# A pooled-attention and maxout kernel: one third of the key folds as a tensor_reduce on VectorE, and a new hand-written order of all steps

## The chip, the cores and the metric

The kernel runs on one core of a Trainium2 chip. The metric is the device time of one execution in microseconds (us), median of the runs shown. The profile is one further execution, taken by the hardware profiler; its span runs from the first to the last instruction. TensorE's granted clock was 1.000 of full speed over the profiled span.

## The reference, cut to what matters

Keys and values are averaged over groups of 8 tokens, so that 576 tokens attend to 72 pooled keys; the attention output goes through a maxout layer of three weights and an output projection.

```python
k_p = k.reshape(B, H, Sp, pool, D).mean(axis=3)     # B=8, H=8, S=576, pool=8, Sp=72, D=64
v_p = v.reshape(B, H, Sp, pool, D).mean(axis=3)
scores = scale * np.matmul(q, k_p.transpose(0, 1, 3, 2))
attn = softmax(scores)                               # over the 72 pooled keys
x = np.matmul(attn, v_p)  -> [4608 tokens, 512]
h = np.maximum(np.maximum(x @ w1, x @ w2), x @ w3)   # 512 -> 768
out = h @ w_out                                      # 768 -> 512
```

## The kernel before, in words

Two streams are interleaved. The **attention stream** goes batch by batch (8 batches of 576 tokens), the **maxout stream** goes in blocks of 512 tokens (9 blocks, 0 to 8). Batch b+1 is attended to while block b goes through the maxout layer, since a block needs the tokens of its batch.

For a batch, Pool (GpSimd) issues the loads of k, q and v (`load_k` L79, `load_q` L99, `load_v` L91). The average over 8 tokens is made as a "fold": three additions that halve the 8 neighbours each time, 8 to 4 (L163), 4 to 2 (L165), 2 to 1 (L167). For batch 1 VectorE folds the keys (`fold_k(b, nc.vector)`), for batches 2 to 7 Pool does, and Pool folds the values of all batches but the first. The folded keys `kp` are transposed on TensorE (`keys`, tile `pkt`, L202) and copied to `kz` by VectorE and ScalarE (`turn_k`, L213). The queries are transposed on TensorE (tiles `pqt`, L195) for batches 0 to 2, and by one DMA transpose on SP's queue (step `T`, L349, into `qT`) for batches 3 to 7. Scores (L226, tiles `psc` and `psf`) go to ScalarE for exp (L231). `values` multiplies with the folded values (tile `pav`, L302), and VectorE normalises (reciprocal L310, product L312, tile `xn`). `turn_x` transposes `xn` into the ring `xT`: on TensorE (tile `pxt`, L293) for batches 0 to 2, by DMA transposes on SP's queue (L287) from batch 3 on.

For a block, `hidden` makes 12 pieces of 4 matmuls (tile `pw`, L419); ScalarE evicts the first of each pair with relu (L425), VectorE the second with a max (L427, tile `hT`). From block 1 the output projection is done with seven products in the place of eight (`out_seven`, L765, tiles `oA`, `oB`, `oC`); its sums of token and hidden tiles are made by VectorE (`sums_of`, L664, tile `tt`), and its evictions by ScalarE (L776) and VectorE (L779). From block 6 the maxout matmuls use the same scheme (`seven`, L842), on weight sums `sw` made earlier by VectorE (`fold_w`, L588 and L597).

The order on every engine is the order in which the program's steps are written out. After block 0 there are two kinds of hand-written lists: `MIDDLE`, one string for each of blocks 1 to 5, and `ORDER`, one string for the rest, run by `weave`. The steps are:

- `h-` and `h+`: the matmuls of the next piece of the block's hidden layer, and its eviction. `-` begins a step and `+` ends it, for all steps; a step without a sign is both.
- `1` to `7` with `-`, `+`: the seven output products (10 matmuls each); `a1` to `a4`, `b1` to `b4`: their sums on VectorE. `f`: one weight sum of `fold_w`. `S`: one sum of output weights (L649).
- `q0` to `q3`, `T`, `k`, `s0`, `s3`, `s6`, `v0` to `v4`, `x0` to `x4`: the attention steps above, of the next batch if no batch is named; `4:T` names batch 4.
- `q4<`, `k4<`, `v4<`: Pool issues a load, behind the last hidden matmuls and the last `T` written so far. `k4+2`, `v3+2`: Pool does the next two steps of a fold. `!`: the next fold step is held until VectorE's last difference of a weight or tile sum has ended.
- In `ORDER`, `1a` is product 1 of the maxout scheme for part a of the block, `o1` an output product, `s70` a score step of batch 7, `v62` and `x62` value steps of batch 6; `b1` to `b4` and `F`, `T`, `H`, `h` are sums and projection pieces.

Where it matters for the prediction: the load of batch 7's queries is `q7<`, its DMA transpose `7:T`, and the first score that reads it `s70`.

Of the kernel before, what the change touches and what calls it, by code (L numbers as in the profile page):

```python
# [14 lines left out]
def kernel(  # L15
# [141 lines left out]
    def fold_steps(e, t, out, dtype=F32, parts=1):  # L157
        part, n = t.shape[:2]
        f = const.tile([part, n, 4, D], dtype, name="half" if dtype == F32 else "halfh",
                       tag="half" if dtype == F32 else "k16")  # L160
# [177 lines left out]
    def do(b, steps):  # L338
# [3 lines left out]
        for name in steps.split():  # L342
# [530 lines left out]
    fold_k(2, nc.gpsimd)  # L873
# [5 lines left out]
    def pool_step(n, name):  # L879
# [69 lines left out]
    MIDDLE = {  # L949
        1: """  # L950
            h- q4< k4< h+ 1:x2 1:v4- h- h- v4< h+ 1:v4+ h+ h- 1:x3 h- h+ h+ h- 1:x4 h+ h- k-
            h- h+ h+ q0 h h- k+ h+ h q1 h s0- s0+ s0+ q2 h- s0+ h- s0+ h+ b1 S q3 h+ h- S S
            3:T S h+ a3 s3- a1 s3+ s3+ h- s3+ h- h+ h+ a2 h- s3+ a4 s6- s6+ 1- s6+ h+ b3 b2
            b4 v0 2- 1+ 6- x0 v1 7- v2- 6+ x1 5- 2+ 7+ v2+ ! k3+4 v3- v3+2 v3+ 5+ v4 3- x2
            4- x3 3+ 4+ x4
        """,
        2: """
            h k5< k- h- k+ h+ a1 a3 h- a2 f a4 f ! v3+2 v5< h+ f s0- s0+ s0+ s0+ h- h- h- h+
            h+ s0+ h- h+ s3- h+ h- f s3+ h- s3+ h+ h- s3+ b1 s3+ s6- h+ s6+ h- h+ h- s6+ !
            k4+2 h+ h+ b2 b3 b4 ! k4+2 1- 4:T v0- 1+ v1- v0+ x0 2- v1+ 6- v2- 7- x1 2+ 7+  # L960
            v4+2 6+ v2+ 5- v3- 5+ v3+ x2 x3 v4 x4 3- 4 3+
        """,
        3: """
            k- q5< k+ a3 k6< h a1 h- h- h+ a2 s0- f a4 ! v4+2 s0+ s0+ f h- h+ s0+ h+ s0+ h-
            h- h+ h+ s3- h- v6< h+ h s3+ s3+ s3+ s3+ h- b1 h- h+ h+ s6- s6+ ! k5+2 h h- s6+
            1- h+ b2 b3 b4 1+ ! k5+2 v5+2 v0- 2- v0+ x0 v1 6- 2+ x1 6+ 7- 5:T 7+ v2- 5- v2+
            x2 v3- 5+ v3+ v4 x3 3 x4 4
        """,
        4: """
            h- q6< h+ k- h- k+ a1 a2 f h+ h- a3 a4 ! v5+2 h- f h+ k7< h+ s0- s0+ h- h- s0+  # L970
            s0+ h+ s0+ h+ 6:T h- s3- h+ s3+ s3+ s3+ h- s3+ h+ h- b1 h+ h ! k6+2 s6- s6+ h h
            b3 b2 b4 s6+ ! k6+2 1- v6+2 v0 2- 1+ x0 v1- 6- v1+ 2+ x1 v2 7- 6+ 5- x2 v3 6:k-
            x3 7+ 5+ 3- 6:k+ v4 x4 4- 3+ 4+
        """,
        5: """
            h q7< a1 v7< h- a2 h- a3 h+ h+ a4 ! v6+2 h- s0- s0+ h+ s0+ h- s0+ s0+ h- h- k7+4
            h+ h+ s3- h+ 7:T s3+ h- s3+ h- s3+ s3+ h+ s6- h+ s6+ s6+ h h- v0 h+ h- x0 v1- h+
            v1+ x1
        """}
    folds = iter([f for wi in range(1, 3) for f in [fold_w(wi)] * 4])  # L980

    def middle(n):

        pieces, outs, out_tiles = hidden(n), None, project(n)
        for name in MIDDLE[n].split():
            if name[0] == "h":
                parts(name, lambda: next(pieces))
            elif name == "F":
                next(out_tiles)
            elif name == "f":  # L990
                next(next(folds))
# [15 lines left out]
    for n in range(1, 6):  # L1007
        middle(n)
# [50 lines left out]
```

## Time and profile before

| what | value |
| --- | --- |
| time, median of 3 runs | 226.8 us (226.77 to 227.67) |
| profiled execution, its own time | 227.08 us |
| its span, first to last instruction | 225.4 us |
| TensorE matmuls, busy | 212.3 us (94% of the span) |
| VectorE, busy | 161.4 us (72%) |
| ScalarE, busy | 120.3 us (53%) |
| Pool, busy | 140.9 us (63%) |
| instructions | 4876 |

A row of the groups of instructions reads: line, engine, operation, output tile and input tiles, shapes (partitions x elements, type), how many; then busy us in total, mean ns of one; then the engine's idle us just before them and what ended most of it. In the timeline, the first number is the start in us, the second the length, and brackets hold the idle time before and what ended it. A line of the waits reads: engine and tile that waited, what it waited for, then us in total, how often, the longest.

### The profile page before, as it was taken

How to read it: one execution, taken by the hardware profiler on the slowest of the kernel's cores; microseconds unless marked ns; L12 is line 12 of the kernel's file. 1: busy time of each engine (PE TensorE's matmuls, PEld its weight loads, DVE VectorE, ACT ScalarE, POOL GpSimd, SP SyncE). 2: the span in 40 equal slices, each digit the busy share in tenths (PEclk: the TensorE clock that was granted, in tenths of full speed). 3: DMA queues.
4: the chain of work that ended last, by engine and by line, in shares of the span. 5: the costliest groups of instructions: out<-in, count | busy, mean ns of one | idle time of the engine just before them, and what ended most of it. 6: DMA issues, size and time to landing. Idle time of an engine off the chain costs nothing.

```text
span 225.4 us, 4876 instructions
## 1 busy us (share of the span) xinstructions
PE 212.3 (94%) x1884; PEld 147.1 (65%) x1885; DVE 161.4 (72%) x314; ACT 120.3 (53%) x233; POOL 140.9 (63%) x121
## 2 busy tenths in 40 slices
PE   6688999999999999999999999999799999999993
PEld 2477744458658645964685468547589667788882
DVE  3668898036997796776679668729767977878940
ACT  2267524855883576237724842693694445564330
POOL 7974300999939969775885769794292903881020
PEclk9999999999999999999999999999999999999999
DMA  6999999999649999649967999699530755200265
GB/s 179 209 197 197 211 203 209 202 168 230 115 105 156 168 176 247 122 61 214 252 85 154 221 202 151 86 236 166 109 56 19 163 102 113 47 0 3 66 198 159
DMA packets 47303, 33.55 MB, mean 149 GB/s; under 512 B 26992, under 2 KB 42288, under 8 KB 47280
## 3 DMA queue, kind: packets, MB, share of 16 engines
q0 software_dynamic: 16944, 16.98, 47.8%
q1 hardware_dynamic: 29888, 15.87, 31.1%
q10 hardware_dynamic: 448, 0.39, 0.7%
q8 instruction: 15, 0.25, 0.5%
q14 instruction: 8, 0.07, 0.1%
HBM read 34.60 MB, written 9.44 MB: 195 GB/s over the span
## 4 chain that ended last, share of the span: by engine, by line
PE 58%; DMA 17%; DVE 10%; POOL 7%; ACT 3%; issue 3%; ACTq 0%; POOLq 0%; DVEq 0%
PE pw L419 17%; PE oA L765 12%; DMA vt<-in_v_dram 8%; PE oC L765 6%; PE pA L842 5%; DMA mw<-in_moe_w_dram 4%; DMA qT<-qb 4%; PE oB L765 3%; PE pC L842 3%; PE pav L302 2%; PE po L471 2%; PE psc L226 2%; POOL half L163 2%; DVE kz L213 2%; DVE tt L664 1%
## 5 line engine op out<-in xcount | busy, mean ns | idle before, releaser
L419 PE MATMUL pw<-xT,mw 128*128 128x512 f16 (+1 forms) x336 | 68.5, 349 | 0.3 <-ACT xT L296 0.2
L419 PEld LDWEIGHTS <-mw 128*128 128x128 f16 x336 | 30.7, 98 | 26.1 <-issue 1.8
L163 POOL TENSOR_TENSOR half<-vt 72x1024 f32<-72x1024 f16 (+1 forms) x12 | 29.1, 2444 | 20.8 <-DMA vt<-in_v_dram 13.3
L427 DVE TENSOR_TENSOR hT<-t,pw 128x512 f16<-128x512 f16 (+1 forms) x42 | 25.3, 608 | 19.1 <-PE pw L419 11.3
L231 ACT ACTIVATE et<-psc 72x512 f16<-72x512 f32 (+2 forms) x66 | 33.9, 571 | 6.7 <-PE psc L226 6.5
L165 POOL TENSOR_TENSOR half<-half 72x1024 f32<-72x1024 f32 (+1 forms) x13 | 28.1, 2165 | 12.6 <-DVE tt L664 5.2
L425 ACT ACTIVATE t<-pw 128x512 f16<-128x512 f32 (+1 forms) x42 | 22.6, 538 | 15.1 <-PE pw L419 14.5
L312 DVE TENSOR_TENSOR xn<-pav,rcp 128x512 f16<-128x512 f32 x40 | 27.6, 691 | 1.4
L776 ACT COPY osb<-oA 128x512 f32<-128x512 f32 x20 | 11.7, 587 | 20.1 <-PE oA L765 19.9
L851 ACT CAST pad<-pA 128x512 f16<-128x512 f32 x27 | 15.1, 585 | 11.7 <-PE pA L842 9.1
L765 PEld LDWEIGHTS <-tt 128*128 128x128 f16 x200 | 18.8, 98 | 2.1
L163 POOL TENSOR_TENSOR half<-ktFalse 96x768 f32<-96x768 f16 (+1 forms) x11 | 19.3, 1773 | 0.6 <-issue 0.5
L226 PEld LDWEIGHTS <-kz 64*128 64x128 bf16 (+1 forms) x161 | 8.9, 95 | 12.4 <-issue 7.2
L302 PEld LDWEIGHTS <-et 72*128 72x128 f16 x320 | 14.9, 98 | 3.0 <-issue 1.1
L302 PE MATMUL pav<-vp,et 72*128 72x65 f16 x320 | 16.3, 194 | 0.6 <-POOL vp L167 0.3
L310 DVE RECIPROCAL rcp<-pav 128x8 f32<-128x8 f32 x40 | 8.1, 201 | 11.3 <-PE pav L302 11.2
L842 PEld LDWEIGHTS <-sw 128*128 128x128 f16 x144 | 13.8, 98 | 2.7 <-issue 0.2
L822 DVE SCALAR_TENSOR_TENSOR hT<-pad 128x512 f16<-128x512 f16 x18 | 14.0, 785 | 1.1 <-ACT pad L855 0.5
L819 DVE TENSOR_TENSOR pad<-pad,pC 128x512 f16<-128x512 f16 x18 | 12.3, 681 | 3.5 <-PE pC L842 2.7
L226 PE MATMUL psc<-qT,kz 64*128 64x256 bf16 (+5 forms) x138 | 13.3, 263 | 1.0 <-DVE qT L197 0.9
L616 POOL TENSOR_TENSOR pad<-xT 128x256 f16<-128x256 f16 x8 | 5.5, 687 | 13.1 <-DMA xT<-xn 13.1
L765 PEld LDWEIGHTS <-hT 128*128 128x128 f16 x126 | 12.3, 98 | 1.4
(122 smaller groups left out, 400.6 us busy)
## 6 DMA issues: line engine op xcount, KB each, us to landing
out_dram<-osb SPq DMA_DIRECT2D x32, 128.0 KB, 4.6
ktFalse<-in_k_dram POOLq DMA_DIRECT2D x7, 576.0 KB, 9.1
qb<-in_q_dram POOLq DMA_DIRECT2D x7, 576.0 KB, 7.6
vt<-in_v_dram POOLq DMA_DIRECT2D x7, 576.0 KB, 11.8
out_dram<-osb SPq DMA_DIRECT2D x11, 256.0 KB, 6.8
mw<-in_moe_w_dram POOLq DMA_DIRECT2D x9, 256.0 KB, 9.2
ktTrue<-in_k_dram SPq DMA_DIRECT2D x3, 384.0 KB, 5.1
out_dram<-ob SPq DMA_DIRECT2D x8, 128.0 KB, 2.9
```

Source lines behind the costliest of these rows:

```text
L163: yield e.tensor_tensor(out=f[:, at], in0=t[:, at, 0:4, :], in1=t[:, at, 4:8, :], op=ALU.add)
L165: yield e.tensor_tensor(out=f[:, :, 0:2, :], in0=f[:, :, 0:2, :], in1=f[:, :, 2:4, :], op=ALU.add)
L226: nc.tensor.matmul(out, kz_all[b % 2][f % 2][rows, h, :], qTs[b][rows, n + i0:n + i1, 64 * (h % 2):64 * (h % 2) + 64], start=True, stop=True)
L231: nc.scalar.activation(out=out, in_=in_, func=FT.Exp, scale=1.0 / 64.0)
L302: nc.tensor.matmul(pav[:, h // 4, 65 * (h % 4):65 * (h % 4) + 65], ets[b][:, h, c0:c0 + 128], vp_all[:, b, h, :], start=True, stop=True)
L312: nc.vector.tensor_tensor(out=xn, in0=pv[:, :, :, 0:D], in1=rcp.to_broadcast([128, 2, 4, D]), op=ALU.mult)
L419: mm = nc.tensor.matmul(pw, w_sb[wi][:, kc, bass.ts(jc, 128)], x[:, kc], start=(kc == 0), stop=(kc == KCH - 1))
L425: yield lambda t=t, pw=pw: nc.scalar.activation(out=t, in_=pw, func=FT.Relu)
L427: yield lambda t=t, pw=pw: nc.vector.tensor_tensor(out=hT[:, jc, c0:c1], in0=t, in1=pw, op=ALU.max)
L765: nc.tensor.matmul(p, left, right, stop=(r == 4), skip_group_check=True, start=(i in FIRST and r == 0 and (m == 0 or n == LAST)))
L842: mm = nc.tensor.matmul(p[:, w], a[:, kc, bass.ts(g, 128)], b[:, kc, :], start=(i in FIRST and w + kc == 0), stop=(w + kc == 2), skip_grou ...
L851: nc.scalar.copy(out=kept(i, g), in_=p)
```

## The change

1. A new function `reduce_k` makes the pooled keys of two of the six key rows per partition (`i` 0 and 1 of 6) with one VectorE instruction, a `tensor_reduce` over the 8 neighbours, 96 x 1024 elements in, 96 x 128 out. It is called as step `K0` for batches 2 to 7. Pool's fold of those batches covers the other four rows, in 3 instructions (96 x 1024, 96 x 512, 96 x 256 elements written) where there were 4 (for batch 2, where there were 3, also 3).
2. `MIDDLE` becomes one list for blocks 1 to 5. A step names its block (`3/h-`) or batch (`4:T`), so that steps of neighbouring blocks may stand between each other. All its steps stand in a new order, and 3 of the key fold steps stand behind a `!` where 7 did.
3. `ORDER` is written anew: the same steps in another order.

The matmuls are the same in number and shape. Block 0 and all that comes before the first `MIDDLE` step are the same, but for Pool's fold of batch 2.

```diff
+    def reduce_k(b, i0, i1):
+        if b not in kps:
+            new_kp(b)
+        with nc.allow_low_precision(reason="summed in f32, rounded once as stored"):
+            nc.vector.tensor_reduce(out=kps[b][:, i0:i1],
+                                    in_=kts[b][:, i0:i1].rearrange("p i j d -> p i d j"),
+                                    op=ALU.add, axis=mybir.AxisListType.X)
...
+            elif name[0] == "K" and b > 1:
+                reduce_k(b, 2 * i, 2 * i + 2)
...
-    fold_k(2, nc.gpsimd)
+    fold_k(2, nc.gpsimd, 2, 6)
...
-                folding[what, b] = fold_steps(nc.gpsimd, kts[b], kps[b], parts=2)
+                folding[what, b] = fold_steps(nc.gpsimd, kts[b][:, 2:6],
+                                              kps[b][:, 2:6], parts=1)
...
     ORDER = """
-        b1 o1- 2a- b3 o1+ k7- b2 1a- 1b- v62- 1a+ k7+ 2a+ b4 T o6- s70- o6+ o2- s70+ o2+ 6a-
...
+        b1 o1- 1a- b3 b2 k7- v62- o1+ k7+ b4 1b- 1a+ 2a- T 2a+ o6- o2 7a 6a- 1b+ o6+ s70 v62+
...
-        2: """
-            h k5< k- h- k+ h+ a1 a3 h- a2 f a4 f ! v3+2 v5< h+ f s0- s0+ s0+ s0+ h- h- h- h+
-            h+ s0+ h- h+ s3- h+ h- f s3+ h- s3+ h+ h- s3+ b1 s3+ s6- h+ s6+ h- h+ h- s6+ !
-            k4+2 h+ h+ b2 b3 b4 ! k4+2 1- 4:T v0- 1+ v1- v0+ x0 2- v1+ 6- v2- 7- x1 2+ 7+
-            v4+2 6+ v2+ 5- v3- 5+ v3+ x2 x3 v4 x4 3- 4 3+
-        """,
-        3: """
-            k- q5< k+ a3 k6< h a1 h- h- h+ a2 s0- f a4 ! v4+2 s0+ s0+ f h- h+ s0+ h+ s0+ h-
...
-        5: """
-            h q7< a1 v7< h- a2 h- a3 h+ h+ a4 ! v6+2 h- s0- s0+ h+ s0+ h- s0+ s0+ h- h- k7+4
...
+    MIDDLE = """
+        2:q0 1/h- 2:K0 1/h+ v4< q4< k4< 1:v4- 1:x2 3:T 1/h 1:v4+ 1/h- k3+1 1/h+ 1:x3 1/h 2:k-
...
+        2/b4 v4+2 3:v0+ 2/6- 3:v1- q5< 3:v1+ 2/6+ 3:x0 2/7 2/2+ 3:v2- 3:x1 2/5- 3:v2+ 3:v3-
+        3:v4- 3:x2 2/5+ 3:v3+ 3:v4+ 2/3 2/4- 4:k- 3/a3 3/h- 3/a1 3/h- 3/h+ 4:k+ 3/h- k6< 3/a2
...
+        5:s6+ 4/1+ 4/b4 4/2- 5:v0 4/6 5:v1- 5:x0 5:v1+ 4/2+ 5:v2 4/5- 5:v3- ! k6+2 5:v3+ 4/7-
+        v6+2 q7< 5:v4- 5:x1 4/5+ 4/7+ 5:x2 5:v4+ 4/3- 5:x3 4/4- 6:k- 5/h- 6:k+ 4/4+ 5/h- 5/h+
+        5/h- ! v6+2 7:K0 5/h+ v7< k7+1 5/a1 6:s0- 6:s0+ 5/h+ 6:s0+ 6:s0+ 5/a2 5/h- 5:x4 6:s0+
+        7:T 5/h+ 5/h 5/h- 6:s3- 6:s3+ 6:s3+ 5/h+ 5/a3 6:s3+ 5/h- 5/h- 6:s3+ 5/h+ 6:s6- 6:s6+
...
```

More of the change, by code (lines that the diff above doesn't have):

```diff
@@ L158, in fold_steps @@
         part, n = t.shape[:2]
[L159 to L160 removed]
+        f = const.tile([part, 6 if part == 96 else n, 4, D], dtype, name="half" if dtype == F32 else "halfh",
+                       tag="half" if dtype == F32 else "k16")[:, 0:n]
         for i in range(0, n, n // parts):
@@ L991, in middle @@
+    """
+    folds = iter([f for wi in range(1, 3) for f in [fold_w(wi)] * 4])
+    def middle():
+        pieces, outs = {}, {}
+        for name in MIDDLE.split():
+            n, _, step = name.rpartition("/")
+            n = int(n or 0)
+            if step[0] == "h":
+                if n not in pieces:
+                    pieces[n] = hidden(n)
+                parts(name, lambda: next(pieces[n]))
+            elif step == "f":
                 next(next(folds))
-            elif name == "!":
+            elif step == "S":
+                next(out_sums)
+            elif step == "!":
@@ L1004, in middle @@
-        assert next(pieces, None) is None
+            elif n and step[0].isdigit():
+                if n not in outs:
+                    outs[n] = out_seven(n)
+                parts(name, lambda: outs[n](int(step[0]), 0, 1))
+            elif step[0] in "ab":
+                sums_of(n, step)
+            elif step[2:3] == "<" or step[2:3] == "+" and step[3:]:
+                pool_step(step)
+            else:
+                b, _, step = step.rpartition(":")
+                do(int(b), step)
@@ L1006 @@
+        assert all(next(p, None) is None for p in pieces.values())
     tt_all.append(const.tile([128, 4, 5, HALF], F16, name="tt", tag="tt"))
-    for n in range(1, 6):
-        middle(n)
+    middle()
     assert next(folds, None) is None
```

82 lines of the change are left out of this document (32 added, 50 removed).

## The prediction

> **What bounds the kernel now.** I read the busy shares first, then TensorE's busy time by stage, then what TensorE waited for, then the timeline at its gaps.
>
> ```profile
> PE 212.3 (94%) x1884; PEld 147.1 (65%) x1885; DVE 161.4 (72%) x314; ACT 120.3 (53%) x233; POOL 140.9 (63%) x121
> ```
>
> TensorE's matmuls fill 94% of the span, so a faster fold can't pay by itself: Pool (63%) and VectorE (72%) are not the bound. Only TensorE's idle time can be won. The busy time by stage says where that lies (each line: stage and its length, then matmuls, weight loads, VectorE, ScalarE, Pool, each with its instructions, granted clock, DMA share, GB/s):
>
> ```profile
> 45.00:60.00 15.00, 14.50 (x157) 10.37 (x154) 9.61 (x23) 8.85 (x19) 14.60 (x10) 1.00 0.99 189
> 60.00:80.00 20.00, 19.66 (x189) 13.37 (x187) 17.01 (x32) 12.76 (x26) 15.95 (x12) 1.00 0.73 136
> 80.00:100.00 20.00, 19.85 (x172) 13.02 (x170) 16.27 (x33) 9.48 (x19) 16.36 (x12) 1.00 0.80 155
> ...
> 155.00:160.00 5.00, 3.40 (x40) 2.84 (x38) 4.13 (x9) 2.70 (x5) 0.00 (x0) 1.00 1.11 165
> 160.00:175.00 15.00, 14.49 (x159) 12.81 (x158) 11.09 (x23) 10.35 (x20) 8.42 (x5) 1.00 0.22 40
> 175.00:185.00 10.00, 9.28 (x81) 6.71 (x80) 9.27 (x15) 3.90 (x8) 5.64 (x8) 1.00 0.62 134
> 185.00:220.00 35.00, 35.00 (x311) 29.69 (x309) 27.05 (x45) 17.54 (x35) 13.80 (x18) 1.00 0.29 73
> ```
>
> Length less matmul time is TensorE's idle time: 0.50, 0.34, 0.15, then (100 to 120, 120 to 140, lines not shown) 0.25 and 0.28, none from 140 to 155, then 1.60, 0.51, 0.72, none to 220. Together 4.35 us. The 8 us or so of idle time before 45 us (start, first loads) and after 220 us (last stores) lie in parts that the change leaves alone. So 226.8 less 4.35, some 222.5, is a floor. The largest gap, in the list of waits and in the timeline (start, length, what; brackets: idle before and what ended it):
>
> ```profile
> PE psf L226 <- DMA qT<-qb: 1.6, 1, 1.6
> ```
>
> ```profile
> 150.51 7.15 SPq L349 DMA_TRANSPOSE qT<-qb  x1
> ...
> 153.96 0.99 POOL L167 TENSOR_TENSOR kp<-half 96x384 bf16<-96x384 f32 x1
> ...
> 155.72 0.29 PE L202 MATMUL pkt<-ident,kp 96*128 96x96 bf16 x3
> ...
> 159.85 0.38 PE L226 MATMUL psf<-qT,kz 128*128 128x320 bf16 x2 [1.60 <-DMA qT<-qb]
> ```
>
> Batch 7's queries come late: their DMA transpose is issued at 150.51, and TensorE stands still for 1.60 us. The other two lines show how close Pool is: batch 7's pooled keys are done at 154.95 and read at 155.72, 0.77 us later.
>
> **The reduce.** Per batch it removes a third of Pool's fold. Rows of the groups, shapes kept apart:
>
> ```profile
> L163 POOL TENSOR_TENSOR half<-ktFalse 96x768 f32<-96x768 f16 x10 | 16.2, 1639 | 0.6 <-issue 0.5
> L165 POOL TENSOR_TENSOR half<-half 96x768 f32<-96x768 f32 x6 | 10.8, 1807 | 5.2 <-DVE rcp L310 5.0
> L167 POOL TENSOR_TENSOR kp<-half 96x384 bf16<-96x384 f32 x6 | 6.0, 993 | 0.5
> L427 DVE TENSOR_TENSOR hT<-t,pw 128x512 f16<-128x512 f16 x30 | 20.5, 685 | 17.1 <-PE pw L419 9.7 <-ACT t L425 4.2 <-ACT et L231 3.0
> L427 DVE TENSOR_TENSOR hT<-t,pw 128x256 f16<-128x256 f16 x12 | 4.8, 416 | 2.0 <-PE pw L419 1.6 <-ACT t L425 0.4
> ```
>
> A fold costs Pool 2 x 1.64 + 1.81 + 0.99 = 6.1 us now and about two thirds, 4.1 us, after: 12 us less in six batches. By itself that is worth nothing, as no TensorE wait above 0.3 us is put down to Pool; it is slack. VectorE gets six tensor_reduces of 1024 elements in. No row shows one, so I bound it. From 256 to 512 elements L427 grows by 269 ns, so 1024 elements cost 685 + 2 x 269 = 1.22 us. The half-size inputs at the fast pace (L664: 512 f16 in 418 ns, 768 in 568) would give 0.72 us. I take 1.22, since the eight neighbours lie 64 elements apart, unlike those of the fast rows: 6 x 1.22 = 7.3 us. The upper end is a reduce held up by Pool, which the timeline shows for another VectorE operation:
>
> ```profile
> 59.31 2.67 POOL L165 TENSOR_TENSOR half<-half 72x1024 f32<-72x1024 f32 x1
> ```
>
> ```profile
> 59.69 2.58 DVE L649 TENSOR_TENSOR so<-wm 128x512 f16<-128x512 f16 x1
> ...
> 63.61 0.41 DVE L649 TENSOR_TENSOR so<-wm 128x512 f16<-128x512 f16 x1
> ```
>
> The same sum takes 2.58 us beside a running Pool addition and 0.41 us beside none, so 2.2 us of blocking: a reduce so held costs 3.4 us, six of them 20. The Trainium skill, page "SBUF — State Buffer", section "Who interferes with whom", says that a VectorE operation with two SBUF inputs is held by a Pool operation that reads SBUF, and that a tensor_reduce never is on this chip; by that rule the upper end falls away and the sum is 7.3. Its page "VectorE: DVE Perf Modes", section "The perf-mode tier table", speaks against the change: a tensor_reduce runs one element a cycle whatever the type, and it advises against it on a hot path; at that page's 0.96 GHz 1024 elements are an estimate of 1.07 us before the fixed part, so the sum stays near 7. Without these sentences the sum goes by 1.22 and both ends stay in the range.
>
> What hides 7.3 us: VectorE's own idle time. At 60 to 80 us it is busy 17.01 of 20, at 80 to 100 16.27 of 20; one to two reduces a stage fit on average. Locally they don't all. `2:K0` stands in front of batch 1's last normalisation, whose transposes TensorE needs at once: I charge **+0.3 us** (0 to 1.2). If the cover is gone elsewhere, each costs up to its 1.22.
>
> **The new order.** Each moved step is judged at the gap that it touches.
>
> *Batch 7's queries* (the 1.60). Here `q7<` opens block 5 and waits for its first hidden matmuls (issue 142.89, with 0.96 us of idle time ended by `pw`). In the new list it stands in block 4's tail, behind `v6+2`, where those matmuls are long done: the 0.96 goes, and Pool, which comes to it past a key fold that is 2 us shorter but held by a later sum, is about 1 us sooner: 1.9 us earlier in all. `s70` has moved past `o2` (10 matmuls, 1.09 us in the chain of waits), `7a` and `6a` (4 matmuls each, 0.44): 1.96 us later. So the transpose has 3.8 us more room, and 1.6 was short. SP's queue is free as much earlier for `x60`, which waited behind it. What is late next is the copy of batch 7's keys to `kz` by ScalarE behind VectorE (157.05 to 159.01 now), needed by the same bank's next product: I leave 0.3. **-1.3 us.**
>
> *160 to 175* (0.51, one wait of a score for exp, L231): `v64` and `3a` (0.27 + 0.44 of matmuls) now stand in front of `s75`, where `v64` alone stood between `s74+` and `s76-`. **-0.3.** *175 to 185* (0.72: 0.40 of it product `4c` waiting for an addition L819, 0.24 a value step waiting for a normalisation): `3c` now stands between `7c` and `4c`, and `6a` between `v72+` and `v73-`, 0.44 us of matmuls each. **-0.4.** *60 to 140* (0.34, 0.15, 0.25, 0.28): four of these are the second copy of bank `oA` by ScalarE (0.15 to 0.3 each), and the new list keeps that sequence of products, so I take **-0.2**, from the 0.34.
>
> The blocking above falls too: at 59 to 63 VectorE lost 2.2 + 0.5 us to Pool. Pool starts batch 3's keys unheld now, but its `q4<` still waits for `3:T` (issue 67.12 now), so the four `S` and most of the `a` sums stand in Pool's idle time. That pays for two reduces there; `b4` may meet the key fold instead (up to 1.3 us). I take no gain.
>
> *A new tight place*: between the matmuls of `3:v2` and the next block's first `pw`, which reads what `3:x2` wrote, there stood products 7, 5, 3, 4 (1.09 each), `v3`, `v4` (0.27 each) and `k` (0.13), 5.0 us; now 5, 3, 4 and the rest, 3.9 us. The way is 0.20 + 0.69 on VectorE, then a 1.2 us transpose on SP that lands 2.4 us after issue: 3.3 us, and behind `2+` on VectorE 0.6 more. It just fits: **+0.2** (0 to 1.3).
>
> **Sum**: -1.3 - 0.3 - 0.4 - 0.2 + 0.3 + 0.2 = -1.7. Small gaps under 0.1 us (issue of a weight load, some 0.2 in all) may go as well: -1.9. The profiled execution took 227.08, so 225.2; the median of the runs is 0.28 lower: **224.9 us**. About 0.5% (1.1 us, to 225.7 or 227.9) is what a measurement of this kernel can tell from no change.
>
> **Rivals.**
>
> - *A, forecast*: 224.9, own range 223.7 to 225.7. For it: the largest gap has a named cause, and the move frees twice what is missing. Chance 0.55.
> - *B, gaps move*: the seam at 155 to 160 stays short, because q6, T6, q7, T7 run one behind the other and transposes varied from 2.0 to 7.2 us on SP; half of the 1.6 comes back, and the block 1 and block 3 charges are 0.5 each: 226.4. 0.20.
> - *C, slower*: VectorE becomes the bound in blocks 1 to 3. Place: `2:K0` to `4:K0`, each in front of a normalisation that TensorE waits for. At 60 to 65 and 80 to 85 us VectorE is busy all the time, which speaks for it; that Pool's blocking falls there speaks against it. It decides when VectorE reaches the normalisation of `3:v2` more than 0.6 us after its matmuls. Price: three reduces on the path, 3.7 us, less the seam's 1.6: 228.9. 0.17.
> - *D, more*: all of the idle time from 155 to 185 goes (2.8) and half of the rest (0.7): 223.3. 0.08.
> - That the reduce does not do what it says (0.7 or 3.4 us each) is inside C and D.
>
> Faster by over 0.5%: A almost whole and D, 0.62. Within: B and A's edge, 0.21. Slower: C, 0.17. The range 223.2 to 228.0 leaves out most of C and the low edge of D.
>
> **What would show it.** Right: no wait of `psf` for `qT`, the transpose issued with more than 10 us before its reader; six VectorE rows of about 1.2 us; Pool busy near 129 us; idle time at 155 to 185 under 1.2 us. Wrong: `psf` or `pA` still waiting there; reduces over 2 us; VectorE above 9.5 of 10 us for a stretch with TensorE waiting on `xn`, or a wait of `pw` for `xT` as block 3 begins.

## The result and the profile after

The changed kernel takes **237.9 us** (median; 236.7 to 241.5) beside 226.8 us: 1.046 times as long, 95% interval 1.039 to 1.054. The ratio is taken from the means of the runs within 1.5% of each kernel's fastest, which leaves out 241.5 us. The forecast was 224.9 us and the range ended at 228.0. The profiled execution took 238.95 us, its span 237.1 us, 11.7 us more than before's 225.4.

The busy line of the page after, and the two longest waits of TensorE once the hand-written lists run (waiter, what it waited for, us in total, times, longest):

```profile
PE 216.3 (91%) x1885; PEld 147.8 (62%) x1885; DVE 175.1 (74%) x320; ACT 120.6 (51%) x233; POOL 128.2 (54%) x116
```

```profile
PE pw L430 <- issue: 7.9, 1, 7.9
PE pw L430 <- DVE hT L438: 2.6, 1, 2.6
```

Pool works 12.7 us less, near the 129 us forecast. Its three rows of a key fold, in the columns of the groups, add up to 4.2 us:

```profile
L163 POOL TENSOR_TENSOR half<-ktFalse 96x1024 f32<-96x1024 f16 x6 | 12.8, 2129 | 0.2
...
L165 POOL TENSOR_TENSOR half<-half 96x512 f32<-96x512 f32 x6 | 8.0, 1338 | 8.4 <-DVE tt L675 5.0 <-DVE sw L599 3.2
...
L167 POOL TENSOR_TENSOR kp<-half 96x256 bf16<-96x256 f32 x6 | 4.4, 735 | 0.5
```

But TensorE, which never waited for more than 1.6 us there in the kernel before, now stands still twice. By stage, for the kernel before (first fence) and after (second), in the columns of the prediction's table. The stages are stretches of time, so behind the first stop the same stage holds earlier work in the changed kernel:

```profile
115.00:120.00 5.00, 4.84 (x61) 4.30 (x60) 3.54 (x8) 1.35 (x3) 4.84 (x4) 1.00 0.73 122
120.00:125.00 5.00, 5.00 (x32) 2.31 (x30) 4.58 (x11) 3.03 (x7) 1.36 (x3) 1.00 0.70 118
125.00:130.00 5.00, 5.00 (x30) 2.09 (x29) 2.56 (x5) 4.25 (x10) 4.44 (x4) 1.00 1.13 270
```

```profile
115.00:120.00 5.00, 4.84 (x63) 4.33 (x61) 3.74 (x9) 1.64 (x3) 4.53 (x3) 1.00 1.64 126
120.00:125.00 5.00, 0.72 (x9) 0.52 (x6) 1.06 (x2) 0.12 (x1) 0.00 (x0) 1.00 1.26 98
125.00:130.00 5.00, 1.42 (x4) 0.59 (x5) 1.41 (x4) 0.00 (x0) 0.00 (x0) 0.61 1.32 169
...
155.00:160.00 5.00, 3.89 (x27) 1.81 (x27) 4.97 (x4) 3.82 (x9) 4.46 (x4) 1.00 1.42 211
160.00:175.00 15.00, 13.14 (x115) 9.11 (x115) 12.51 (x26) 7.68 (x16) 3.35 (x3) 1.00 0.85 121
```

From 120 to 130 us every engine nearly stands still while the DMA engines are busy and move few bytes (share 1.26, 98 GB/s). That is the head of block 4. The chain of waits names the transfer (start, length from issue to landing, what), and the timeline shows what went before on SP (the first row holds three transposes, issued at 106.22, 114.07 and 115.37), on Pool and on TensorE:

```profile
114.07 12.43 DMA xT<-xn
```

```profile
106.22 13.00 SPq L296 DMA_TRANSPOSE xT<-xn  x3
119.33 8.99 SPq L358 DMA_TRANSPOSE qT<-qb  x1
```

```profile
102.04 0.54 POOL L79 DMA_DIRECT2D ktFalse<-in_k_dram  x1 [2.02 <-PE pw L430]
...
107.48 0.87 POOL L91 DMA_DIRECT2D vt<-in_v_dram  x1
```

```profile
128.58 4.00 PE L430 MATMUL pw<-xT,mw 128*128 128x512 f16 x9 [7.86 <-issue]
```

Block 4's first `pw` reads what `3:x3`, `3:x4`, `4:x0` and `4:x1` transpose. The last two are issued at 114.07 and 115.37 us, as early as before (113.96, 115.27), and land after 12.4 and 13.1 us (before: 2.4 and 4.0). The list of waits has no name for the end of this wait ("issue"), but `pw` starts 0.09 us after `4:x1` landed, here as in v6_moved, v6_mid and v6_behind below. `3:x4` is late too: issued at 106.22, it lands at 125.07, 4.4 us after TensorE began to wait at 120.72. By the trace's packets, batch 6's keys and values were on their way at the same time: k6 from 105.8 to 118.3 us (before: 104.6 to 108.4), v6 from 114.1 to 125.7 (before: 110.0 to 114.4). In the kernel before both loads fell between the transposes of batch 3 (last issue 99.00) and of batch 4. The new order leaves `3:x4` until 106.22, 0.5 us after k6's load begins, and from there the traffic is jammed until 128 us.

To compare kernels I use **lost time**: how much later a matmul starts than the columns of all matmuls ahead of it would have it, at 0.215 us for 512 columns (the trace's spacing of back-to-back ones). The stretches are given in us of matmul work done, so they are the same work in each kernel; 41 is early in block 1, 106 to 112 the head of block 4, 132 to 142 the first half of block 5, 142 to 203 the last batch and the blocks after it. The forecast's gains lie in the last stretch.

| lost us by stretch of work | 41-66 | 66-106 | 106-112 | 112-132 | 132-142 | 142-203 | sum |
| --- | --- | --- | --- | --- | --- | --- | --- |
| before | 1.40 | 0.84 | 0.12 | 0.17 | -0.16 | 4.28 | 6.65 |
| after | 1.64 | 1.17 | **10.17** | 0.37 | **2.54** | **2.04** | 17.93 |
| x_first | 1.64 | 1.06 | 0.02 | 0.37 | 4.18 | 2.04 | 9.31 |
| x_k7 | 3.61 | 1.09 | 0.02 | 0.37 | -0.10 | 2.55 | 7.54 |
| k3_b4 | 1.65 | 1.08 | 0.02 | 0.36 | -0.07 | 2.54 | 5.58 |
| repaired_no_reduce | 2.27 | 1.19 | 0.02 | 0.37 | -0.17 | 4.05 | 7.73 |
| reduce_only | 2.14 | 0.84 | 0.12 | 0.17 | -0.16 | 4.43 | 7.54 |

So the new order did gain 2.2 us in the last stretch, and lost 10.1 and 2.7 us at two other places.

The second place: VectorE's sums `5/a1`, `5/a2` beside Pool's fold of batch 7's keys, in the timeline after:

```profile
156.16 0.87 POOL L91 DMA_DIRECT2D vt<-in_v_dram  x1 [0.44 <-issue]
...
156.39 3.07 DVE L675 TENSOR_TENSOR tt<-xT 128x512 f16<-128x512 f16 x1
...
157.04 2.13 POOL L163 TENSOR_TENSOR half<-ktFalse 96x1024 f32<-96x1024 f16 x1
...
159.25 1.33 POOL L165 TENSOR_TENSOR half<-half 96x512 f32<-96x512 f32 x1
159.50 1.37 DVE L675 TENSOR_TENSOR tt<-xT,tt 128x512 f16<-128x512 f16 x1
```

Sums of 0.41 us take 3.07 and 1.37; each ends 0.3 us after a Pool addition ends (159.47 after 159.18, 160.87 after 160.59). By these records the first sum begins 0.65 us ahead of the fold, while Pool issues a load. The `hT` behind them comes late, and TensorE waits 2.6 us.

### The profile page after: what moved, and what is told of

Same layout as the page of the kernel before. It is cut to its first block, busy times and chain, and to the rows that moved or that the text cites. A ratio compares the mean times of both kernels' runs of the same rounds, so it can differ in the third digit from the quotient of the medians.

```text
span 237.1 us, 4877 instructions
## 1 busy us (share of the span) xinstructions
PE 216.3 (91%) x1885; PEld 147.8 (62%) x1885; DVE 175.1 (74%) x320; ACT 120.6 (51%) x233; POOL 128.2 (54%) x116
## 4 chain that ended last, share of the span: by engine, by line
PE 69%; DVE 12%; DMA 9%; issue 5%; ACT 1%; POOL 1%; DVEq 0%; ACTq 0%; POOLq 0%
PE pw L430 22%; PE oA L776 9%; PE pA L853 6%; DMA xT<-xn 5%; PE oC L776 5%; PE po L482 4%; DMA vt<-in_v_dram 4%; PE pC L853 3%; PE psc L235 3%; DVE xn L321 3%; PE po L478 3%; DVE tt L675 3%; PE oB L776 2%; PE pm L417 2%; PE pav L311 2%
## 5 line engine op out<-in xcount | busy, mean ns | idle before, releaser
L430 PE MATMUL pw<-xT,mw 128*128 128x512 f16 (+1 forms) x336 | 70.6, 356 | 10.8 <-issue 7.9
L430 PEld LDWEIGHTS <-mw 128*128 128x128 f16 x336 | 31.3, 99 | 39.0 <-issue 15.5
L165 POOL TENSOR_TENSOR half<-half 72x1024 f32<-72x1024 f32 (+1 forms) x13 | 24.5, 1888 | 12.5 <-DVE tt L675 8.7
L787 ACT COPY osb<-oA 128x512 f32<-128x512 f32 x20 | 11.7, 587 | 17.0 <-PE oA L776 16.9
L99 POOL DMA_DIRECT2D qb<-in_q_dram x9 | 7.1, 785 | 23.1 <-PE pw L430 11.3
L311 PEld LDWEIGHTS <-et 72*128 72x128 f16 x320 | 14.4, 98 | 2.8 <-DVE xn L321 0.8
L833 DVE SCALAR_TENSOR_TENSOR hT<-pad 128x512 f16<-128x512 f16 x18 | 14.9, 836 | 1.1 <-ACT pad L866 0.8
L675 DVE TENSOR_TENSOR tt<-xT 128x512 f16<-128x512 f16 x10 | 8.7, 877 | 8.0 <-DMA xT<-xn 8.0
L235 PE MATMUL psc<-qT,kz 64*128 64x256 bf16 (+5 forms) x138 | 13.1, 263 | 0.6 <-DVE qT L206 0.6
## 6 DMA issues: line engine op xcount, KB each, us to landing
qb<-in_q_dram POOLq DMA_DIRECT2D x7, 576.0 KB, 10.2
vt<-in_v_dram POOLq DMA_DIRECT2D x7, 576.0 KB, 11.3
```

The costliest lines, as they stand in the source:

```text
L165: yield e.tensor_tensor(out=f[:, :, 0:2, :], in0=f[:, :, 0:2, :], in1=f[:, :, 2:4, :], op=ALU.add)
L235: nc.tensor.matmul(out, kz_all[b % 2][f % 2][rows, h, :], qTs[b][rows, n + i0:n + i1, 64 * (h % 2):64 * (h % 2) + 64], start=True, stop=True)
L311: nc.tensor.matmul(pav[:, h // 4, 65 * (h % 4):65 * (h % 4) + 65], ets[b][:, h, c0:c0 + 128], vp_all[:, b, h, :], start=True, stop=True)
L430: mm = nc.tensor.matmul(pw, w_sb[wi][:, kc, bass.ts(jc, 128)], x[:, kc], start=(kc == 0), stop=(kc == KCH - 1))
L675: gate[:] = [nc.vector.tensor_tensor(out=part[:, int(name[1]) - 1], in0=a, in1=b, op=ALU.subtract)]
```

## The experiments

Theory 1: transposes and loads in flight together hold each other up; that is the head of block 4. Theory H: Pool's folds hold VectorE's two-input sums; that is the second place. Rivals: R, the six reduces make VectorE late; O, the new order comes too late whatever is loaded.

**x_first**: `3:x3` and `3:x4` go ahead of the loads.

```diff
-        2/b4 v4+2 3:v0+ 2/6- 3:v1- q5< 3:v1+ 2/6+ 3:x0 ...
-        3:v4- 3:x2 2/5+ 3:v3+ 3:v4+ 2/3 2/4- ... k6< 3/a2
-        3/h+ 3/h+ 3:x3 2/4+ f ... 5:K0 3:x4 4:s3- ...
+        2/b4 v4+2 3:v0+ 2/6- 3:v1- 3:v1+ 2/6+ 3:x0 ...
+        3:v4- 3:x2 2/5+ 3:v3+ 3:x3 3:v4+ 3:x4 q5< 2/3 2/4- ... k6< 3/a2
+        3/h+ 3/h+ 2/4+ f ... 5:K0 4:s3- ...
```

> The changed kernel with its last two transposes of batch 3 (3:x3 and 3:x4) right behind 3:v3+ and 3:v4+, and q5< behind them; all else as changed. SP then issues the five transposes of batch 3 ahead of the loads of q5, k6 and v6, as the kernel before does, and k6's load has no transpose beside it. Theory 1 (a key or value load and a DMA transpose that run at once both crawl; k6's load beside 3:x4 held back v6's load, and that ran beside 4:x0 and 4:x1, for which TensorE waits 8 us as block 4 begins): k6's load takes about 4 us again instead of 12.5, v6's is over before 4:x0 is issued, the 10.2 us that block 4 loses go, and the time is about 228 (227 to 230). Rival R (the six reduces, 1.92 us each instead of 1.22, make VectorE late): the loss stays, 236 to 239. Rival O (in the new order 4:x1 is issued too late for the first pw of block 4, whatever the loads do): TensorE waits at the same place, less the crawl, 231 to 236.

Measured: 1.010 times before (1.007 to 1.014), 229.8 us beside 227.7. k6's load takes 6.1 us, v6's runs from 111.7 to 117.5, and the loss at 106-112 is 0.02 instead of 10.17 us. Theory 1 holds and R falls for this place; two details are not as expected, since k6's load was to take 4 us and v6's to be over before `4:x0` is issued (114.21). O does not fall by this run, which issues `3:x3` and `3:x4` earlier too; it falls by v6_behind below. The loss in block 5 stays.

**order_only**: the new order without the reduce (all `K0` steps out, Pool folds six rows).

```diff
-    fold_k(2, nc.gpsimd, 2, 6)
+    fold_k(2, nc.gpsimd)
...
-                folding[what, b] = fold_steps(nc.gpsimd, kts[b][:, 2:6],
-                                              kps[b][:, 2:6], parts=1)
+                folding[what, b] = fold_steps(nc.gpsimd, kts[b],
+                                              kps[b], parts=1)
...
-        2:q0 1/h- 2:K0 1/h+ v4< ...
+        2:q0 1/h- 1/h+ v4< ...
```

> The changed kernel without the reduce: the six K0 steps are gone and Pool folds all six rows of each key, in three steps as in the changed kernel; the order of all other steps is the new one. Theory 1 (transposes that run beside key and value loads): the loads stand where they stood, so the loss at the head of block 4 stays, 234 to 241. Rival R (the reduces make VectorE late): 225 to 229. Rival O (the order by itself issues 4:x1 too late): 234 to 241 as well.

Measured: 248.4 us in the middle (239.8 to 249.2; no ratio, since the runs lie too far apart). The loss at 106-112 is there (10.3 us), so R is out once more. Three of the four runs, the profiled one among them, are slower than any of the changed kernel (248.3 to 249.2); the fourth (239.8) is not. In the profile 12.1 us are lost at 41-66, where Pool's fold of batch 3's keys, gated by nothing, holds sum after sum. Two things differ there from the changed kernel, and this run does not separate them (v4_back below has the earlier start with four rows, and loses 4.4 us more there): the fold is longer (6.0 us instead of 4.1), and it starts at 66.83 us instead of 72.81, since `3:T` is issued in 2.04 us instead of 6.67.

```profile
65.83 0.41 DVE L675 TENSOR_TENSOR tt<-xT,tt 128x512 f16<-128x512 f16 x1
66.16 4.06 DVE L675 TENSOR_TENSOR tt<-xT 128x512 f16<-128x512 f16 x1
...
66.83 3.10 POOL L163 TENSOR_TENSOR half<-ktFalse 96x1536 f32<-96x1536 f16 x1
...
70.01 1.87 POOL L165 TENSOR_TENSOR half<-half 96x768 f32<-96x768 f32 x1
70.14 2.02 DVE L675 TENSOR_TENSOR tt<-xT,tt 128x512 f16<-128x512 f16 x1
```

**reduce_only**: the old order with the reduce (`K0` ahead of each key fold, four rows on Pool).

```diff
+    def reduce_k(b, i0, i1):
...
-            h- q4< k4< h+ 1:x2 ...
+            h- 2:K0 q4< k4< h+ 1:x2 ...
...
-            k4+2 h+ h+ b2 b3 b4 ! k4+2 1- ...
+            k4+2 h+ h+ b2 b3 b4 ! k4+1 1- ...
```

> The kernel before with the reduce alone: rows 0 and 1 of the keys of batches 2 to 7 as one tensor_reduce on VectorE, Pool folds the other four rows in three steps; the order of all other steps is the old one. Theory 1: six reduces of 1.9 us on an engine that is idle for a quarter of the time cost little, 226 to 228. Rival R: 232 to 238. Rival O: as theory 1.

Measured: 1.001 (0.998 to 1.005). In the old order the reduce is worth nothing, and it costs nothing that the times show; the profiled execution loses 0.9 us more by the table.

**v6_late** and **v6_moved**: the kernel before with the load of batch 6's values late. In v6_late the old `v6<` stays in, so that it loads twice.

```diff
-            1- h+ b2 b3 b4 1+ ! k5+2 v5+2 v0- ...
+            1- h+ b2 b3 b4 1+ v6< ! k5+2 v5+2 v0- ...
```

v6_moved has this edit and takes the old one out:

```diff
-            h- h+ h+ s3- h- v6< h+ h s3+ ...
+            h- h+ h+ s3- h- h+ h s3+ ...
```

> The kernel before with one step moved: v6< (the load of batch 6's values) from the middle of block 3's scores to behind 1+, just ahead of Pool's second k5+2, so that it is issued at about 112 to 113 us instead of 107.5 and runs while SP issues 4:x0, 4:x1 and 5:T (113.96 to 119.7 in the profile of the kernel before). Nothing else changes, VectorE has no reduce. Theory 1: the load takes 8 to 12 us instead of 4.4, 4:x1 lands late, TensorE waits 4 to 9 us as block 4 begins, 231 to 236. Rivals R and O: the load has time until about 140 us, no change, 226.5 to 227.5.

> The kernel before with v6< taken away from the middle of block 3's scores and put behind 1+, just ahead of Pool's second k5+2. The run named v6_late left the first v6< where it was, so that batch 6's values were loaded twice, once at 107.5 us as before and once more beside 4:x0, 4:x1 and 5:T; this one loads them once, late. Theory 1 (load and transpose that run at once both crawl): the one load takes 8 to 12 us, TensorE waits 4 to 8 us as block 4 begins, 231 to 235. If it was the double load that cost the time (twice the bytes, the second writing what is still being read): 226.5 to 228.

Measured: v6_late 1.032 (1.023 to 1.040), 7.9 us lost at 106-112; v6_moved 1.007 (1.004 to 1.011), only 1.8 us lost. Neither theory had v6_moved right: its load takes 5.5 us, not 8 to 12. It is issued at 111.5, 2.6 us ahead of `4:x0`; the second load of v6_late is issued at 117.3, behind `4:x0`, `4:x1` and `5:T`. Doubled bytes or the moment of the issue: v6_mid below.

**v6_behind** and **v4_back**: the changed kernel with one load moved, v6_behind:

```diff
-        ... ! v4+2 v6<
+        ... ! v4+2
-        ... 4:x0 4:x1 5:T 3/6- ...
+        ... 4:x0 4:x1 5:T v6< 3/6- ...
```

and v4_back:

```diff
-        ... v4< q4< k4< 1:v4- ...
+        ... q4< k4< v4< 1:v4- ...
```

> The changed kernel with one step moved: v6< from ahead of 3:x4 to behind 5:T, so that batch 6's values are loaded after 4:x0, 4:x1 and batch 5's queries have been transposed. 3:x4 and k6's load stay as changed and still run at once at 106 us. Theory 1a (v6's load beside 4:x0 and 4:x1 is what TensorE waits for): 4:x1 lands 3 to 5 us after its issue instead of 12.4, block 4 loses under 2 us at its head instead of 10.2, and the time is 228 to 231. Theory 1b (k6's load, which crawls from 105.8 to 118.3 us beside 3:x4, alone is enough to hold 4:x0 and 4:x1): block 4 still loses 3 to 8 us, 232 to 237. Rival O (the new order issues 4:x1 too late, whatever is loaded): 236 to 239.

> The changed kernel with v4< behind q4< and k4< again, as the kernel before has them, so that batch 4's values are not loaded beside 3:T. Theory P (what set off the loss at the head of block 4 is Pool's queue, which is 4.4 us late from 71 us on because q4< waits 9.5 us for a 3:T that crawls beside v4's load): q4, k4 and k5 are issued 3 to 4 us earlier, k6's load is over before 3:x4, and block 4 loses under 2 us. Theory 1 as so far (the place of 3:x4 in the order, not Pool's lateness): 3:T lands 3 to 4 us earlier, q4 and k4 are issued earlier, but k6< still waits for its own place in the order at 102 us, runs beside 3:x4, and block 4 still loses 7 to 11 us. Under both, Pool's fold of batch 3's keys, which is gated by nothing, then runs at 67 to 72 us beside tensor_tensors of batch 1 and holds some of them: 0 to 4 us lost between 66 and 75 us that the changed kernel does not lose.

Measured: v6_behind 1.027 (1.023 to 1.031). k6's load still crawls beside `3:x4` (108.2 to 120.5 us), but block 4 loses 2.1 us instead of 10.2, about what theory 1a said (under 2), and O is out; `3:x4` lands at 122.85, just before TensorE is done with the work ahead (123.09). The total is higher than theory 1a said: beside the changed kernel, the late loads behind `5:T` cost 2.7 us more at 127-132, and a sum held for 3.06 us costs 2.1 us more at 61-66. v4_back: 243.2 us (one run). `3:T` is issued in 1.94 us instead of 6.67 and q4 comes 5.3 us earlier, yet block 4 loses the same 10.2 us: theory P is out. The earlier fold then costs 4.4 us more than in the changed kernel at 41-66 (5.99 against 1.64), a little over the 4 allowed.

**v6_mid**: the kernel before, v6 loaded once, behind `k5+2`.

```diff
-            h- h+ h+ s3- h- v6< h+ h s3+ ...
-            1- h+ b2 b3 b4 1+ ! k5+2 v5+2 v0- ...
+            h- h+ h+ s3- h- h+ h s3+ ...
+            1- h+ b2 b3 b4 1+ ! k5+2 v6< v5+2 v0- ...
```

> The kernel before with its one load of batch 6's values (v6<) moved behind Pool's second k5+2, so that it is issued at about 116 us, when 4:x0 and 4:x1 (113.96 and 115.27) have been issued and 5:T follows. If the moment counts (a load that comes while transposes are in flight holds them up for as long as it runs): TensorE waits 4 to 8 us as block 4 begins, 231 to 235. If the 7.9 us of v6_late came from loading twice: under 2 us, 226.5 to 229, as in v6_moved.

Measured: 1.024 (1.021 to 1.027), 5.6 us lost at 106-112. Issued at 116.06, the load takes 6.8 us. SP's timeline of v6_mid, then of x_first, where v6's load (111.7 to 117.5 us) is nearly over when `5:T` is issued:

```profile
113.96 2.52 SPq L287 DMA_TRANSPOSE xT<-xn  x2
116.58 8.08 SPq L349 DMA_TRANSPOSE qT<-qb  x1
```

```profile
114.21 2.53 SPq L296 DMA_TRANSPOSE xT<-xn  x2
116.84 3.33 SPq L358 DMA_TRANSPOSE qT<-qb  x1
```

So it is the moment: one load that comes while transposes are in flight holds them up. `4:x1` lands at 123.58 us, 4.3 us later than in the kernel before. With no change but this in the kernel before, it makes half of the changed kernel's loss. What the other 2.3 us of v6_late are (its first load also takes 6.5 us instead of 4.5) was not separated. How little room there is shows in x_first: there `4:x1` lands at 120.46, and `pw` starts on time at 120.70.

**x_k7** and **x_k7_v7**: x_first with batch 7's fold behind the sums, then also its values behind `7:T`. The edit of x_k7 on x_first:

```diff
-        5/h- ! v6+2 7:K0 5/h+ v7< k7+1 5/a1 ...
-        k7+2 6:s6+ 5/h- 5/h+ 5/a4 5/h- ...
+        5/h- ! v6+2 7:K0 5/h+ v7< 5/a1 ...
+        6:s6+ 5/h- 5/h+ 5/a4 ! k7+3 5/h- ...
```

and of x_k7_v7 on x_k7:

```diff
-        ... 7:K0 5/h+ v7< 5/a1 ...
-        7:T 5/h+ 5/h 5/h- ...
+        ... 7:K0 5/h+ 5/a1 ...
+        7:T v7< 5/h+ 5/h 5/h- ...
```

> x_first with Pool's fold of batch 7's keys moved: k7+1 and k7+2 go from behind v7< and from the end of batch 6's scores to one k7+3 behind 5/a4, gated by it. Theory H (in x_first the two tensor_tensors of 5/a1 and 5/a2 take 3.12 and 1.37 us instead of 0.41, since Pool's key fold at 147.05 to 151.46 holds them, and TensorE waits 2.7 us for the hT behind them, then runs some us at a lower granted clock): the two take 0.4 to 0.6 us, the stage from 140 to 160 gets 2.5 to 4 us back, and the time is 0.988 to 0.997 of before, that is 224 to 226.5. Rival V (the reduce 7:K0 of 1.91 us right ahead, at 143.94, is what makes VectorE late there): the wait for hT shrinks by less than 1 us, ratio 1.003 to 1.012. Rival L (batch 7's keys come late for the weave when they are folded at about 153 us): a new wait of 1 to 3 us for kp or kz past 160 us, ratio 1.000 to 1.010.

> x_k7 with v7< moved from ahead of 5/a1 to behind 7:T, so that batch 7's values are loaded when its queries have been transposed instead of beside them. Theory 1: 7:T's issue on SP takes 3 to 6 us instead of 9.7 and v7's load 4.4 to 5.5 us instead of 8.8. TensorE waits for neither in x_first, so the time is that of x_k7 within 0.4%. If batch 7's queries or batch 6's tiles, which are transposed behind 7:T, do hold the end of the middle: up to 1.5 us less. If v7 comes too late for vpool: up to 2 us more.

Measured, x_k7: 0.999 (0.996 to 1.002). The two sums are back at 0.4 us, with `7:K0` where it was, so rival V is out:

```profile
148.30 0.87 POOL L91 DMA_DIRECT2D vt<-in_v_dram  x1 [0.45 <-DVE kp L182]
...
148.50 0.41 DVE L675 TENSOR_TENSOR tt<-xT 128x512 f16<-128x512 f16 x1
...
148.94 0.43 DVE L675 TENSOR_TENSOR tt<-xT,tt 128x512 f16<-128x512 f16 x1
...
154.50 2.11 POOL L163 TENSOR_TENSOR half<-ktFalse 96x1024 f32<-96x1024 f16 x1 [5.33 <-issue]
```

The issue of a load beside them does not hold them. The stretch 132-142 falls from 4.18 to -0.10 us. The total did not fall as far, because this execution loses 2.0 us more at 41-66 than x_first: one sum held for 2.93 us by the ungated `k3+1`. x_first has the same order there and was spared, and x_k7's twelve runs spread from 225.8 to 229.8. x_k7_v7: 1.021 (1.017 to 1.025), not the same as x_k7. `7:T` is issued in 3.26 us instead of 8.50, as said, but `v7<` now waits 8.8 us at the head of Pool's queue, batch 7's fold waits behind it, and TensorE waits 3.3 us for `kp`.

**k3_late**, **best**, **k3_b4**, **k3_b4_v4**: x_k7 with batch 3's fold behind the last `S`, or behind `1/b4`, each without and with the swap of v4_back. First what all four take out, then where k3_late and best put it, then k3_b4 and k3_b4_v4:

```diff
-        ... 1:v4+ 1/h- k3+1 1/h+ ... 1:x4 k3+2 1/h- ... 2:q1 1/h- v3+2 1/h- ... k5< 2:s0- ...
+        ... 1:v4+ 1/h- 1/h+ ... 1:x4 1/h- ... 2:q1 1/h- 1/h- ... 2:s0- ...
```

```diff
-        ... 1/a4 S 1/h- ...
+        ... 1/a4 S ! k3+3 v3+2 k5< 1/h- ...
```

```diff
-        1/b4 2:v1+ 1/6- ...
+        1/b4 ! k3+3 v3+2 k5< 2:v1+ 1/6- ...
```

> x_k7 with Pool's fold of batch 3's keys and the first half of its values' fold (k3+1, k3+2, v3+2) and k5< moved from the middle of block 1 to behind its last S, gated by it. In x_k7 an ungated k3+1 at 70.54 us holds one tensor_tensor for 2.93 us, and TensorE loses 2.3 us there. Theory H (a two-input tensor_tensor on VectorE waits for the Pool fold that runs beside it): that loss goes and nothing else changes, 0.986 to 0.994 of before, that is 224 to 226. Rival L (Pool's later steps, v3's second half, k4 and the loads behind them come late instead): 0.995 to 1.005.

> k3_late with v4< behind q4< and k4< again. Theory P: 3:T, no longer beside v4's load, is issued in 2 to 3 us instead of 6.7, q4 and k4 are loaded 3 to 4 us earlier; TensorE waits for none of these, so the time is that of k3_late within 0.4%, 0.985 to 0.994 of before. Rival L: Pool's queue, less late, ends the loss that k3_late still has, up to 1 us less. If the earlier k4 or q5 meets other transposes: 0.995 to 1.02.

> x_k7 with k3+1, k3+2, the first v3+2 and k5< moved behind 1/b4, the last sum of block 1 that VectorE makes, and gated by it (k3_late put them behind the last S, with the tensor_tensors of 1/b2 to 1/b4 still to come). Theory H (the loss at 66 to 75 us is Pool's ungated fold holding those tensor_tensors): no tensor_tensor before 80 us takes over 0.8 us, TensorE loses under 0.7 us between 61 and 66 us of its work in every run, the times no longer fall into two groups, and the ratio is 0.990 to 0.997. Rival: the fold comes too late for the keys of batch 3, whose kp and kz then hold TensorE at 80 us by 1 to 3 us, 1.000 to 1.012.

> k3_b4 with v4< behind q4< and k4<, so that batch 4's values are not loaded beside 3:T. In the run named best the same swap made 3:T's issue 1.97 us instead of 2.3 and brought q4 and k4 3.9 us forward, and Pool's fold of batch 3's keys with them into tensor_tensors that it held for 4.7 us in all. Theory H: behind 1/b4 the fold can't meet them, so the time is that of k3_b4 within 0.4%, 0.988 to 0.997. If the earlier loads themselves cost the 4 us in best: 1.01 to 1.02 again.

Measured: k3_late 1.000 (0.997 to 1.004), best 1.016 (1.013 to 1.020). Both miss: the gate was the last `S`, and the sums `1/b2` to `1/b4` come after it. With the swap (best) the fold starts at 68.05 us and holds three of them (2.25, 1.62, 2.43 us). That k3_late misses for the same reason is not shown: its profiled execution (226.8 us) holds no sum before 80 us, while its runs spread from 226.0 to 229.4. Behind `1/b4`: k3_b4 **0.9965** (0.994 to 0.999), its runs together within 226.1 to 227.9, and k3_b4_v4 0.997 (0.994 to 0.999). No sum before 80 us is held in either, so the swap by itself does nothing, as Theory H said. k3_b4 is faster than the changed kernel by some 5%, and than the kernel before by 0.35%, with an interval that just leaves out no change.

**repaired_no_reduce**: k3_b4_v4 without the reduce, by the edit of order_only.

> k3_b4_v4 without the reduce: the six K0 steps are gone and Pool folds all six rows of each key in the same three steps, 6.0 us instead of 4.1. Theory as in the prediction (the reduce by itself is worth nothing, it costs VectorE 1.92 us a batch and Pool gains 2): within 0.5% of k3_b4_v4. Rival H (the longer ungated folds k4+1, k5+1 and k6+1 hold more tensor_tensors, as they did in order_only): 1 to 4 us more.

Measured: 1.008 (1.005 to 1.011). The reduce is worth 1.1% in this order (1.008 to 0.997), where the prediction had nothing. Without it TensorE waits 3.1 us for `kp`, which Pool finishes late, and ten sums take 0.8 to 2.1 us. This holds against folds of six rows in three long steps; folds cut in halves, as in the kernel before, were not tried in this order.

**red_flat**: x_first with the reduce summing eight adjacent numbers, which are not the sums that the kernel needs; only its time is of use.

```diff
-                                    in_=kts[b][:, i0:i1].rearrange("p i j d -> p i d j"),
+                                    in_=kts[b][:, i0:i1].rearrange("p i j d -> p i (j d)").rearrange(
+                                        "p i (d j) -> p i d j", j=8),
```

> x_first with the reduce reading its 96 x 1024 numbers as 128 groups of eight neighbours instead of eight numbers that lie 64 apart: the same count in and out, other sums, so the outputs of batches 2 to 7 are not the reference's. If the stride makes the reduce 1.9 us instead of the 1.22 that the prediction took, its six rows fall to 1.0 to 1.3 us. If it is the reduce as such (one number at a time from either layout), they stay at 1.85 to 1.95.

Measured (one run, 227.7 us): the rows of the reduce in the changed kernel and in red_flat:

```profile
L182 DVE TENSOR_REDUCE kp<-ktFalse 96x128 bf16<-96x1024 f16 x6 | 11.5, 1918 | 0.0
```

```profile
L182 DVE TENSOR_REDUCE kp<-ktFalse 96x128 bf16<-96x1024 f16 x6 | 7.2, 1207 | 0.0
```

So it is the stride: 1.21 us for neighbours, 1.92 us for numbers that lie 64 apart.

## Why the prediction was wrong, step by step

- **The step that failed: "Each moved step is judged at the gap that it touches."** The gaps were those of the kernel before. The steps that did the harm, `q5<`, `k6<`, `v6<`, `3:x3` and `3:x4`, touch none of them: their order was turned round, and the sum has no term for it. Its price was 10.05 us (10.17 less 0.12). x_first turns the order back and the loss goes; v6_behind moves v6's load alone and is left with 2.1 us, so most of the price is that load beside `4:x0` and `4:x1`, with `3:x4` still on its way; v6_mid makes half of it in the kernel before. The trace of before had a hint: `4:T`, `6:T` and `7:T`, each beside a load (of k5, k7, v7), took 5.52, 5.91 and 7.15 us to issue, `3:T` and `5:T`, alone, 1.96 and 3.11. The prediction only said that "transposes varied from 2.0 to 7.2 us" and did not ask what ran beside them.
- **Pool as slack.** The hold of 2.2 us on a sum was found and used as a bound for the reduce, and for one place ("`b4` may meet the key fold instead (up to 1.3 us)"). It was not carried to the other folds that lost their `!`. At `k7+1` it cost 2.7 us (2.54 against -0.16) in the changed kernel, and at `k3+1` it comes and goes (0 to 2.1 us with the order as changed) with the moment at which `3:T` lands, for which `q4<` ahead of the fold waits on Pool.
- **The reduce** was priced at 1.22 us, from rows whose elements are adjacent; it takes 1.92. For adjacent elements the figure is right (red_flat: 1.21 us); the prediction named the stride, but had no term for it, and it adds 0.71 us. The upper end (held by Pool, 3.4 us) did not occur: in the changed kernel all six take 1.90 to 1.94 us, among them some that run beside Pool additions almost throughout. That agrees with the rule that the prediction took from the Trainium skill, "SBUF — State Buffer", section "Who interferes with whom". The 4.2 us too few were covered by VectorE's idle time (reduce_only 1.001).
- **"By itself that is worth nothing"**: right in the old order (reduce_only), wrong in the new one, where it is worth 1.1% once the jams are mended.
- **The gains of the new order** (-2.0 us from 155 to 185) came: 142-203 loses 2.04 us instead of 4.28 in the changed kernel, 2.54 in k3_b4. `psf` no longer waits for `qT`. In k3_b4, whose span is 225.1 us, the stages lie where they lay before:

```profile
155.00:160.00 5.00, 4.20 (x46) 3.59 (x45) 4.95 (x11) 1.70 (x4) 1.44 (x2) 1.00 0.97 190
160.00:175.00 15.00, 15.00 (x163) 13.26 (x162) 12.44 (x23) 11.21 (x22) 8.82 (x6) 1.00 0.33 59
175.00:185.00 10.00, 9.93 (x92) 7.21 (x91) 9.31 (x16) 5.17 (x9) 4.91 (x7) 1.00 0.60 137
```

  TensorE's idle time falls there from 1.60, 0.51 and 0.72 us to 0.80, 0.00 and 0.07: 0.8, 0.5 and 0.65 us gained where 1.3, 0.3 and 0.4 were forecast. The sum is right and its terms are not, which is luck. The first is short by the wait for the copy of batch 7's keys, for which the prediction left 0.3 us; it is 0.8.
- **The small charges** held in size, but not where they were laid. 41-66 loses 0.24 us more (0.3 was charged for `2:K0` in front of a normalisation); at 54 us TensorE waits 0.4 us for the keys that `2:K0` makes, and for no normalisation. 66-106 loses 0.33 more (0.2 charged for the tight place at block 3's head); block 3's first `pw` waits for nothing, and a value step at 96.25 us waits 0.5 us for a normalisation. The 0.2 us hoped for from 60 to 140 did not come.
- **Rival C** had the sign and not the cause: VectorE at `2:K0` to `4:K0` loses no more than those charges. With the jam and the held sums mended, k3_b4 comes out at -1.07 us of lost time (5.58 less 6.65) and 0.35% in the timed runs, where -1.9 was forecast. That is inside the 0.5% which the prediction called no change.

The changed kernel's sum, from the table: 0.24 + 0.33 + 10.05 + 0.20 + 2.70 - 2.24 = 11.3 of the 11.7 us by which the span grew.

What stays open: why the DMA engines share as they do. k6's load in the changed kernel ran beside a transpose and stores of the output, and which of the two slowed it more was not separated.

## What to carry to other kernels

When an order is rewritten, list for every transfer what will be in flight beside it, loads against transposes above all: a step that waits for nothing today may be safe only because of the steps between which it stands. Do the same for Pool: a fold without a gate may start at any time within several us, and every two-input sum of VectorE that it can meet is a sum that may take as long as the fold. A change with good parts can hide behind one bad seam; a table of lost time by stretch of the same work shows which part did what.

## What the runs showed of the hardware

- **A load that comes while DMA transposes are in flight.** A 576 KB load of values takes 4.5 us by its packets when alone (v6 before). It takes 5.8 us when its packets begin 2.5 us ahead of the issue of `4:x0` (x_first, 0.02 us lost), 5.5 us when they begin 1.0 us ahead (v6_moved, 1.8 lost), and 6.8 us when they begin behind it (v6_mid, 5.6 lost); in the changed kernel, where k6's load is jammed already, 11.7 us (10.2 lost). The transposes of `4:x0` and `4:x1` land there after 12.4 and 13.1 us, where 2.4 is the median of all 27 such transposes before. The Trainium skill, page "DMA: Bandwidth & Descriptors", section "Rules for kernel authors", says that a transpose next to ordinary DMAs needs nothing; no run here shows that it needs anything for its result, but for its time it needs room.
- **After a long wait TensorE is slow as well.** The nine matmuls after the wait of 7.9 us take 4.00 us, where nine such took 2.10 at 99.64 us: they start 0.43 us apart instead of 0.22, and the granted clock reads 0.61 from 125 to 130 us. Of the 10.17 us lost, an estimated 2.3 are this (10.17 less 7.86). The Trainium skill, page "TensorE: Matmul & The Clock Gate", section "What's actually happening", has the clock at half rate after an idle window of about 3.4 us until one such window was busy; the rows agree.
- **A held sum ends 0.3 us after the Pool instruction beside it**, and the next may be held by the next: 4.06, then 2.02 us beside Pool's 3.10 and 1.87, where 0.41 is the time alone. By the records some of these sums begin up to 0.7 us ahead of the fold that holds them (66.16 and 66.83, 156.39 and 157.04); why is open.
- **A strided reduce** costs 1.6 times one of neighbours (1.92 and 1.21 us for 1024 f16 elements).
